# Key and value caches of a decode kernel: one queue with 64 KB rows, or two queues with 32 KB rows

## The chip, the cores and the metric

The kernel runs on one core of a Trainium2 chip. The metric is the device time of one execution in microseconds (us); lower is better.

## What is computed

One decoding step for a batch of 2: attention of 16 heads over a cache of 4096 positions with heads of 256, mixed by a gate with a small dense block. All is float32.

```
q = (x @ wq)                               # x: 2 x 448, wq: 448 x 4096
scores = q . k_cache * 256**-0.5           # per batch and head: 4096 scores
p = softmax(scores)
o = p . v_cache                            # per batch and head: 256 numbers
a = o @ wo                                 # wo: 4096 x 448
b = relu(x @ w1) @ w2                      # w1: 448 x 1792, w2: 1792 x 448
g = sigmoid((x * gate_w).sum())
out = g * a + (1 - g) * b
```

Each cache is 2 x 16 x 4096 x 256 float32, 134 MB. The two caches are nearly all of the 290 MB that the core reads.

## The kernel before

**Units.** The work is cut into U = 32 units, one for each pair of batch and head. Keys and values of a unit stand together in one input, `kv`: for each unit 128 rows (one for each partition of the on-chip memory) of SW = 16384 float32, which is 64 KB. The first half of a row is keys, the second half values. One DMA brings one unit, 8.39 MB.

**The ring.** On chip there are SLOTS = 3 buffers of 64 KB a partition (`ring`, `slot[0]` to `slot[2]`). Unit u goes to slot (u+1) % 3. Slot 0 first holds `wq` and the small inputs, then unit 2. At the end slot 0 takes `wm` (w1 and w2) after unit 29, and slot 1 takes `wo` after unit 30.

**The queue.** All DMAs are issued by SyncE (SP in the profile), in one queue: `wq`, unit 0, unit 1 at the start; unit 2 once the projections have read `wq` (semaphore `q_mm`); then unit u+3 each time unit u has been used up (semaphore `freed`, counted by VectorE), in a loop (L157 to L163) and written out at the end (L164 to L176). The last unit, 31, comes in two DMAs, keys first (L167, semaphore `slot_in[2]`) and values (L168, `last_v`). Then `wm` in two DMAs and `wo` in six.

**A unit's chain.** TensorE waits for the unit's slot (`slot_in`) and for its query (`queried`), and makes the scores with 32 matmuls of 128x512 (L131, `unit_pe`). VectorE takes the maximum (L351). ScalarE makes the exponentials and their sum (L318) and copies the next unit's query (L320, which releases `queried`). VectorE multiplies the eight blocks of values by the exponentials and adds up (L356), in place in the ring; the last of the eight adds 1 to `freed`. ScalarE copies the eight results (L323, `ov`). ScalarE's loop over units is L316 to L323.

**Start and end.** At the start ScalarE waits for `wq` on `slot_in[0]` (L296), spreads x, and TensorE makes the gate and the queries in two halves (L196 to L211). At the end TensorE has the hidden layer of the dense block (L111), the merge over units, w2 (L258), and `wo` in six blocks (L270, L283), each as it lands.

Each engine's instructions run in the order in which the code below issues them; the engines are held together by semaphores alone.

Of the kernel before, what the change touches and what calls it, by code (L numbers as in the profile page):

```python
# [7 lines left out]
ET = mybir.EngineType  # L8
# [4 lines left out]
SLOTS = 3  # L13
# [4 lines left out]

def gated_mix_decode(nc, wq, kv, wm, wo, out):
    U, _, SW = kv.shape  # L20
    D = 448
    B = 2
    RB = R // B
    T, DH = 2, 256
# [13 lines left out]
    pe, dve, act, pool, sp = nc.tensor, nc.vector, nc.scalar, nc.gpsimd, nc.sync  # L38
# [4 lines left out]
    def ev():  # L43
        sems.append(nc.alloc_semaphore(f"e{len(sems)}"))
        return sems[-1]
# [5 lines left out]
    slot = [ring[:, i * SW:(i + 1) * SW] for i in range(SLOTS)]  # L51

    def sb(name, *shape):
        t = nc.alloc_sbuf_tensor(name, list(shape), F32)
        assert nc.sbuf_base <= first
        return t.ap()
# [3 lines left out]

    out_sem = nc.alloc_semaphore("out_sem")
    slot_in = [ev() for _ in range(SLOTS)]
    last_v, w1_in, w2_in = ev(), ev(), ev()
    wo_in = [ev() for _ in ACC + DIRECT]
    scored, maxed, raised, queried, freed, kept = (ev() for _ in range(6))

    sp.dma_start(slot[0][:, :wq.shape[1]], wq).then_inc(slot_in[0], 16)
    sp.dma_start(slot[1], kv[0]).then_inc(slot_in[1], 16)
    sp.dma_start(slot[2], kv[1]).then_inc(slot_in[2], 16)

    ident = sb("ident", P, P)
    sel = sb("sel", P, R)
# [15 lines left out]
    p = sb("p", P, SG)  # L88
# [16 lines left out]
    def x_of(c, n=R):  # L105
        return xr[:, c].rearrange("p r b -> p (r b)")[:, :n]
# [17 lines left out]
    def unit_pe(k, u_wait, slot_wait, s):  # L124
        pe.wait_ge(slot_in[s], slot_wait)
        pe.wait_ge(queried, u_wait)
        for c in range(SG // CW):
            for t in range(T):
                for g in range(G):
                    lo = t * S + g * SG + c * CW  # L130
                    m = pe.matmul(sc[g * R:(g + 1) * R, c * CW:(c + 1) * CW],  # L131
                                  qc[:, s, t:t + 1].to_broadcast([P, R]), slot[s][:, lo:lo + CW],
                                  start=(t == 0), stop=(t == T - 1))
        m.then_inc(scored, 1)
# [5 lines left out]
    LOOP = -(-U // SLOTS)  # L140
# [10 lines left out]
    with nc.Block(no_gpsimd_drain=True) as block:  # L151

        @block.sync
        def _(_e):
            sp.wait_ge(q_mm, 2)
            sp.dma_start(slot[0], kv[2]).then_inc(slot_in[0], 16)
            with nc.Fori(0, LOOP - 2, engines=(ET.SP,)) as r:  # L157
                u0 = sp.snap(r * SLOTS)
                for k in range(SLOTS):
                    s = (k + 1) % SLOTS  # L160
                    sp.wait_ge(freed, u0 + k + 1)
                    sp.dma_start(slot[s], kv[bass.ds(u0 + k + SLOTS, 1)].rearrange("o p n -> (o p) n")  # L162
                                 ).then_inc(slot_in[s], 16)  # L163
            sp.wait_ge(freed, U - 4)  # L164
            sp.dma_start(slot[1], kv[U - 2]).then_inc(slot_in[1], 16)
            sp.wait_ge(freed, U - 3)
            sp.dma_start(slot[2][:, :SW // 2], kv[U - 1][:, :SW // 2]).then_inc(slot_in[2], 16)  # L167
            sp.dma_start(slot[2][:, SW // 2:], kv[U - 1][:, SW // 2:]).then_inc(last_v, 16)  # L168
            sp.wait_ge(freed, U - 2)
            sp.dma_start(w1, wm[:, :W1]).then_inc(w1_in, 16)  # L170
            sp.dma_start(w2, wm[:, W1:]).then_inc(w2_in, 16)
            sp.wait_ge(freed, U - 1)
            k = 0
            for n, s in zip(ACC + DIRECT, wo_in):
                sp.dma_start(w_o[:, k * D:(k + n) * D], wo[:, k * D:(k + n) * D]).then_inc(s, 16)  # L175
                k += n  # L176
            sp.wait_ge(res_ok, 1)
            sp.dma_start(out, res[0:7 * 15 + 1:7, :]).then_inc(out_sem, 16)
# [13 lines left out]
        def pe_main():  # L192
            pe.wait_ge(x_ok, 1)
            for c in range(KC):
                r = slice(0, P if c < KF else HP)
                m = pe.matmul(pa[:, :1], x_of(c, P) if c < KF else xn[r].rearrange("p r b -> p (r b)"), xg[r, c, B:],  # L196
                              start=(c == 0), stop=(c == KC - 1))
            m.then_inc(gate_mm, 1)
            W = 2 * KF * DH
            for i in range(2):  # L200
                if i:
                    pe.wait_ge(q_ok, i)
                project(pb, slot[0][:, i * NW // 2:(i + 1) * NW // 2], lambda c, g: g * W + c * CW,
                        lambda i: G * W + i * CW, CW, 0, KC).then_inc(q_mm, 1)
                pe.wait_ge(q_ok, i + 1)
                if i:
                    pe.wait_ge(qt_ok, i)
                else:
                    pe.wait_ge(ident_ok, 1)
                for k in range(2 * T):  # L210
                    m = pe.transpose(pc[:, k * P:(k + 1) * P], q[:, k * P:(k + 1) * P], ident)  # L211
                m.then_inc(q_tr, 1)
            with nc.Fori(0, LOOP, engines=(ET.PE,)) as r:
                u0 = pe.snap(r * SLOTS)

                def units(lo, hi):
                    for k in range(lo, hi):
                        unit_pe(k, u0 + (k + 1), r * 16 + (32 if k == SLOTS - 1 else 16), (k + 1) % SLOTS)

                units(0, FULL)  # L220
                with pe.If_lt(pe.to_reg(r), LOOP - 1):
                    units(FULL, SLOTS)
                pe.end_ifs()
# [69 lines left out]

        @block.scalar
        def _(_e):
            act.wait_ge(slot_in[0], 16)  # L296
            act.activation(xr, xg[:, :KF, None, :B].to_broadcast([P, KF, P // B, B]), AF.Copy)  # L297
            act.activation(xn, xg[:, KF:, :B].to_broadcast([P, P // B, B]), AF.Copy)
            act.wait_ge(xl_0, 1)
            for j in range(2):  # L300
                a = act.activation(xl[j * HP:(j + 1) * HP, j], xg[j * HP:(j + 1) * HP, KF:, :B]  # L301
                                   .to_broadcast([HP, RB, B]), AF.Copy)
            a.then_inc(x_ok, 1)
            act.wait_ge(gate_mm, 1)
            act.activation(ge, pa[:, :1], AF.Exp, scale=-1.0).then_inc(gate_ok, 1)  # L305
            for i in range(2):
                act.wait_ge(q_mm, i + 1)
                act.activation(q, pb, AF.Copy, scale=SCALE).then_inc(q_ok, 1)  # L308
                act.wait_ge(q_tr, i + 1)
                a = act.activation(qt[:, i * U // 2:(i + 1) * U // 2, :].rearrange("p (s n) t -> p s t n", s=2),  # L310
                                   pc.rearrange("p (s t x) -> p s t x", s=2, t=T)[:, :, :, ::17], AF.Copy)
                a.then_inc(qt_ok, 1)
            act.wait_ge(qt_ok, 2)
            act.activation(qc[:, 1, :], qt[:, 0, :], AF.Copy).then_inc(queried, 1)
            qf = qc.rearrange("p s t -> p (s t)")
            with nc.Fori(0, U, engines=(ET.Activation,)) as u:  # L316
                act.wait_ge(maxed, u + 1)
                act.activation(p, sc, AF.Exp, bias=nm[:, bass.ds(u, 1)], accum_out=ls[:, bass.ds(u, 1)]  # L318
                               ).then_inc(raised, 1)
                act.activation(qf[:, bass.ds((u + 2) % SLOTS * T, T)],  # L320
                               qt[:, bass.ds(u + 1, 1), :].rearrange("p o t -> p (o t)"), AF.Copy).then_inc(queried, 1)
                act.wait_ge(freed, u + 1)
                act.activation(ov[:, bass.ds(u, 1), :].rearrange("p o j -> p (o j)"), on, AF.Copy).then_inc(kept, 1)  # L323
            act.wait_ge(nb_ok, 1)
            act.activation(e, pc[:U, 0:P:R], AF.Exp, bias=nb, scale=-1.0).then_inc(e_ok, 1)
            act.wait_ge(hid_mm, 1)
            act.activation(hs, pa[:, :FG], AF.Relu, scale=omg).then_inc(hid_ok, 1)
            act.wait_ge(hid_tr, 1)
            act.activation(hr[:, :KF * G, :], pb[:, :KF * P].rearrange("p (k r) -> p k r", r=R), AF.Copy)
            for j in range(2):  # L330
                r = slice(j * HP, (j + 1) * HP)
                a = act.activation(hr[r, KF * G:, :],  # L332
                                   pb[r, KF * P + j * HP:KF * P + (j + 1) * HP].rearrange("p (k r) -> p k r", r=R),
                                   AF.Copy)
            a.then_inc(hr_ok, 1)
# [102 lines left out]
```

## Time and profile before

| | |
|---|---|
| median of 3 runs | 677.36 us (676.78 to 677.59) |
| the profiled execution's own time | 676.38 us |
| its span, first to last instruction | 674.8 us |
| bytes read | 289.54 MB, mean 429 GB/s over the span |
| DMA packets in SyncE's queue | 6080 |
| busy: TensorE, VectorE, ScalarE | 213.0, 339.8, 54.2 us |

The profile is one execution. Its page has the busy time of each engine, the span in 40 slices with the share of time that the 16 DMA engines were busy and the bytes that they moved, the chain of waits that ended last, groups of instructions by line, and the DMA issues. In the rows of an engine's instructions, the times are start and duration in us; in brackets is the idle time ahead and what ended it. A packet is one row of a DMA, or one write of 4 bytes that tells a semaphore that one DMA engine has done its share.

### The profile page before, as it was taken

The page shows a single profiled execution, that of the slowest core. Times are in us where ns is not written, and L with a number is a line of the kernel's source. Part 1 is how long each engine was busy: PE and PEld are TensorE (multiplying, and loading weights), DVE is VectorE, ACT ScalarE, POOL GpSimd, SP SyncE. Part 2 cuts the span into 40 slices and gives each one's busy share as a digit, 9 for nine tenths or more (in the row PEclk, how much of TensorE's full clock was granted, in tenths as well). Part 3 has the DMA queues.
Part 4 walks back from the last instruction along what each step waited for, and adds up shares of the span by engine and source line. Part 5 has one row for each costly group of instructions (what it writes and reads, how often), then busy time and mean ns, then how long its engine had stood idle before and what let it go on. Part 6 is the DMA issues. An engine that isn't in the chain of part 4 may idle for free.

```text
span 674.8 us, 4173 instructions
## 1 busy us (share of the span) xinstructions
PE 213.0 (32%) x1279; PEld 52.0 (8%) x1279; DVE 339.8 (50%) x561; ACT 54.2 (8%) x144; POOL 1.1 (0%) x9
## 2 busy tenths in 40 slices
PE   0633221333332123333321233333222333332455
PEld 0210000000000000000000000000000000000011
DVE  0024566545455665544656654455566445456670
ACT  0110000000000000000000000000000000000110
POOL 0000000000000000000000000000000000000000
PEclk9976567767655676776656677665667767655879
DMA  9999999999999999999999999999999999999997
GB/s 381 427 435 436 435 435 435 435 435 435 435 435 435 435 435 435 435 435 435 431 435 435 435 435 435 435 435 435 435 435 435 435 435 435 435 435 406 420 437 304
DMA packets 6082, 289.59 MB, mean 429 GB/s; under 512 B 704, under 2 KB 832, under 8 KB 1216
## 3 DMA queue, kind: packets, MB, share of 16 engines
q1 hardware_dynamic: 6080, 289.55, 99.3%
q8 instruction: 2, 0.03, 0.0%
HBM read 289.54 MB, written 0.01 MB: 429 GB/s over the span
## 4 chain that ended last, share of the span: by engine, by line
DMA 70%; DVE 12%; PE 9%; issue 6%; DVEq 1%; ACT 1%; SPq 0%; ACTq 0%
DMA ring<-in_kv 65%; DVE ring L356 10%; PE sc L131 9%; DMA ring<-in_wo 4%; DVE nm L351 2%; DVEq L356 1%; ACT p L318 1%; PE z L283 0%; DVEq L348 0%; DVEq L353 0%; PE acc L270 0%; SPq L175 0%; SPq L162 0%; DVEq L351 0%; DVE a_sb L375 0%
## 5 line engine op out<-in xcount | busy, mean ns | idle before, releaser
L356 DVE SCALAR_TENSOR_TENSOR ring<-ring,p 128x1024 f32 x256 | 295.9, 1222 | 54.8 <-ACT p L318 54.8
L131 PE MATMUL sc<-ring,qc 128*32 128x512 f32 x1024 | 182.6, 878 | 417.8 <-DMA ring<-in_kv 417.8
L351 DVE TENSOR_REDUCE nm<-sc 128x1024 f32 x32 | 39.2, 1225 | 236.1 <-PE sc L131 236.1
L131 PEld LDWEIGHTS sc<-ring,qc 128*32 128x32 f32 x1024 | 41.2, 154 | 558.6 <-issue 558.6
L318 ACT ACTIVATE p<-sc,nm 128x1024 f32<-128x1024 f32 x32 | 35.7, 1114 | 257.8 <-DVE nm L351 257.8
L323 ACT ACTIVATE ov<-on 128x8 f32 x32 | 6.7, 208 | 309.0 <-DVE ring L356 309.0
L356 DVE DVE_READ_ACCUMULATOR ring<-ring,p 128x1 f32 x256 | 21.4, 83 | 0.0
L343 DVE TENSOR_SCALAR ge<-ge 128x1 f32<-128x1 f32 x1 | 0.2, 155 | 21.5 <-ACT ge L305 21.5
L196 PE MATMUL pa<-ring,xr 128*128 128x1 f32 x6 | 1.4, 356 | 21.4 <-ACT xl L301 21.4
L375 DVE COPY a_sb<-acc 128x448 f32<-128x448 f32 x1 | 0.6, 625 | 14.7 <-PE acc L270 14.7
L111 PE MATMUL pa<-ring,xr 128*32 128x448 f32 x24 | 4.2, 830 | 11.7 <-DMA ring<-in_wm 11.7
L270 PE MATMUL acc<-ring,oc 128*32 128x448 f32 x52 | 5.9, 544 | 4.7 <-DMA ring<-in_wo 4.7
L111 PE MATMUL pb<-ring,xr 128*32 128x512 f32 x48 | 7.1, 737 | 0.0
L318 ACT ACTIVATION_READ_ACCUMULATOR p<-sc,nm x32 | 6.2, 193 | 0.0
L320 ACT ACTIVATE qc<-qt x32 | 6.1, 192 | 0.0
L258 PE MATMUL acc<-ring,hr 128*32 128x448 f32 x28 | 3.2, 541 | 1.0 <-ACT hr L332 1.0
L196 PEld LDWEIGHTS pa<-ring,xr 128*128 128x128 f32 x6 | 1.4, 326 | 21.4 <-ACT xl L301 21.4
L270 PEld LDWEIGHTS acc<-ring,oc 128*32 128x32 f32 x52 | 1.7, 109 | 8.9 <-issue 5.9
L114 PE MATMUL pb<-ring,xl 128*64 128x512 f32 x8 | 2.2, 618 | 0.0
L297 ACT ACTIVATE xr<-ring 128x384 f32<-128x384 f32 x1 | 0.5, 522 | 18.3 <-DMA ring<-in_wq 18.3
L111 PEld LDWEIGHTS pb<-ring,xr 128*32 128x32 f32 x48 | 1.6, 132 | 3.9 <-issue 3.9
L308 ACT ACTIVATE q<-pb 128x512 f32<-128x512 f32 x2 | 1.2, 598 | 8.6 <-PE pb L114 8.6
(56 smaller groups left out, 23.7 us busy)
## 6 DMA issues: line engine op xcount, KB each, us to landing
ring<-in_kv SPq DMA_DIRECT2D x2, 4096.0 KB, 34.7
ring<-in_wq SPq DMA_DIRECT2D x1, 7174.0 KB, 19.5
ring<-in_wm SPq DMA_DIRECT2D x2, 3136.0 KB, 30.7
ring<-in_wo SPq DMA_DIRECT2D x1, 3136.0 KB, 24.4
ring<-in_wo SPq DMA_DIRECT2D x1, 1792.0 KB, 28.3
ring<-in_wo SPq DMA_DIRECT2D x1, 896.0 KB, 30.0
ring<-in_wo SPq DMA_DIRECT2D x1, 672.0 KB, 31.1
ring<-in_kv SPq DMA_DIRECT2D x31, 39.6
```

Source lines behind the costliest of these rows:

```text
L111: m = pe.matmul(dst[g * R:(g + 1) * R, :n], x_of(c), w[:, at(c, g):at(c, g) + n], start=(c == 0), stop=False)
L114: m = pe.matmul(dst[i * HP:(i + 1) * HP, :n], xl.rearrange("p j r b -> p (j r b)"), w[:, at_last(i):at_last(i) + n], start=False, stop=True)
L131: m = pe.matmul(sc[g * R:(g + 1) * R, c * CW:(c + 1) * CW], qc[:, s, t:t + 1].to_broadcast([P, R]), slot[s][:, lo:lo + CW], start=(t == 0) ...
L196: m = pe.matmul(pa[:, :1], x_of(c, P) if c < KF else xn[r].rearrange("p r b -> p (r b)"), xg[r, c, B:], start=(c == 0), stop=(c == KC - 1))
L258: pe.matmul(acc[g * R:(g + 1) * R, :D], hr[:, k, :], w2[:, k * D:(k + 1) * D], start=(k < G), stop=False)
L270: m = pe.matmul(acc[g * R:(g + 1) * R, :D], o_of(k), w_o[:, k * D:(k + 1) * D], start=False, stop=(k >= n - G))
L308: act.activation(q, pb, AF.Copy, scale=SCALE).then_inc(q_ok, 1)
L318: act.activation(p, sc, AF.Exp, bias=nm[:, bass.ds(u, 1)], accum_out=ls[:, bass.ds(u, 1)]).then_inc(raised, 1)
L320: act.activation(qf[:, bass.ds((u + 2) % SLOTS * T, T)], qt[:, bass.ds(u + 1, 1), :].rearrange("p o t -> p (o t)"), AF.Copy).then_inc(quer ...
L323: act.activation(ov[:, bass.ds(u, 1), :].rearrange("p o j -> p (o j)"), on, AF.Copy).then_inc(kept, 1)
L351: dve.tensor_reduce(nm[:, bass.ds(u, 1)], sc, axis=AX.X, op=ALU.max, negate=True).then_inc(maxed, 1)
L356: m = dve.scalar_tensor_tensor(v, v, 1.0, p, op0=ALU.mult, op1=ALU.mult, accum_out=on[:, j:j + 1])
```

## The change

Keys and values of a unit become two DMAs. Keys of every unit stay in SyncE's queue; values of units 0 to 30 are issued by ScalarE, in ScalarE's own queue. Each DMA then has rows of 32 KB. Both count on the slot's semaphore, so that TensorE waits for 32 per unit and not 16. `wq` has a semaphore of its own (`wq_in`). ScalarE issues the values of units 0 and 1 when `wq` has landed, those of unit 2 behind the copy of the first query, and those of unit u+3 behind its copy of unit u's results (which waits for `freed`). Its loop is unrolled by three units. Of unit 31, the keys come in two DMAs with rows of 16 KB, and the values stay in SyncE's queue.

```diff
-    sp.dma_start(slot[0][:, :wq.shape[1]], wq).then_inc(slot_in[0], 16)
-    sp.dma_start(slot[1], kv[0]).then_inc(slot_in[1], 16)
-    sp.dma_start(slot[2], kv[1]).then_inc(slot_in[2], 16)
+    HW = SW // 2
+
+    def load(eng, u, s, at, n=HW):
+        rows = kv[u] if isinstance(u, int) else kv[bass.ds(u, 1)].rearrange("o p n -> (o p) n")
+        return eng.dma_start(slot[s][:, at:at + n], rows[:, at:at + n])
+
+    sp.dma_start(slot[0][:, :wq.shape[1]], wq).then_inc(wq_in, 16)
+    for u in range(SLOTS - 1):
+        load(sp, u, u + 1, 0).then_inc(slot_in[u + 1], 16)
...
                     sp.wait_ge(freed, u0 + k + 1)
-                    sp.dma_start(slot[s], kv[bass.ds(u0 + k + SLOTS, 1)].rearrange("o p n -> (o p) n")
-                                 ).then_inc(slot_in[s], 16)
+                    load(sp, u0 + k + SLOTS, s, 0).then_inc(slot_in[s], 16)
...
             sp.wait_ge(freed, U - 3)
-            sp.dma_start(slot[2][:, :SW // 2], kv[U - 1][:, :SW // 2]).then_inc(slot_in[2], 16)
-            sp.dma_start(slot[2][:, SW // 2:], kv[U - 1][:, SW // 2:]).then_inc(last_v, 16)
+            for i in range(2):
+                load(sp, U - 1, 2, i * HW // 2, HW // 2).then_inc(slot_in[2], 16)
+            load(sp, U - 1, 2, HW).then_inc(last_v, 16)
...
-            act.wait_ge(slot_in[0], 16)
+            act.wait_ge(wq_in, 16)
+            for u in range(SLOTS - 1):
+                load(act, u, u + 1, HW).then_inc(slot_in[u + 1], 16)
...
+            load(act, 2, 0, HW).then_inc(slot_in[0], 16)
+
+            def unit_act(u, at):
                 act.wait_ge(maxed, u + 1)
...
                 act.wait_ge(freed, u + 1)
                 act.activation(ov[:, bass.ds(u, 1), :].rearrange("p o j -> p (o j)"), on, AF.Copy).then_inc(kept, 1)
+
+            with nc.Fori(0, LOOP - 2, engines=(ET.Activation,)) as r:
+                u0 = act.snap(r * SLOTS)
+                for k in range(SLOTS):
+                    u, s = act.snap(u0 + k), (k + 1) % SLOTS
+                    unit_act(u, (k + 2) % SLOTS * T)
+                    load(act, u + SLOTS, s, HW).then_inc(slot_in[s], 16)
+            unit_act(U - 5, (U - 3) % SLOTS * T)
+            load(act, U - 2, 1, HW).then_inc(slot_in[1], 16)
+            with nc.Fori(U - 4, U, engines=(ET.Activation,)) as u:
+                unit_act(u, (u + 2) % SLOTS * T)
```

How the instructions stand on the two issuing engines follows. A row has the line, the operation, what it writes and reads, and the semaphores that it waits for, by number. Line numbers of the changed kernel are its own: L71 is the DMA in `load`. `ring_49` is the ring.

ScalarE, the start of its program, before. Semaphore e0 is `slot_in[0]`, on which `wq` lands, and e22 is POOL's clearing of `xl`:

```order
L297 ACT_TABLE_LOAD
L297 ACTIVATE xr<-ring 128x384 [waits e0]
L298 ACTIVATE xn<-ring 128x128
L301 ACTIVATE xl<-ring 64x32 [waits e22]
L301 ACTIVATE xl<-ring 64x32
```

The same place after. Semaphore e3 is `wq_in`, and e23 the former e22:

```order
L71 DMA ring_49<-in_kv 128x8192 [waits e3]
L71 DMA ring_49<-in_kv 128x8192
L305 ACT_TABLE_LOAD
L305 ACTIVATE xr<-ring_49 128x384
L306 ACTIVATE xn<-ring_49 128x128
L309 ACTIVATE xl<-ring_49 64x32 [waits e23]
```

Two DMAs now stand first and carry the wait for `wq`, and the load of the activation table, which stood ahead of that wait, is behind it.

ScalarE, one unit in its loop, before. Semaphore e13 is `maxed`, and e16 `freed`; ISA rows compute addresses:

```order
L318 ISA [waits e13]
L318 ACTIVATE p,ls<-sc,nm 128x1024
L320 ISA x2
L320 ACTIVATE qc<-qt 128x2
L323 ISA [waits e16]
L323 ACTIVATE ov<-on 128x8
```

The same unit after, the first of the three in the loop. Semaphore e14 is `maxed`, and e17 `freed`:

```order
L328 ISA [waits e14]
L328 ACTIVATE p,ls<-sc,nm 128x1024
L330 ISA
L330 ACTIVATE qc<-qt 128x2
L333 ISA [waits e17]
L333 ACTIVATE ov<-on 128x8
L71 ISA
L71 DMA ring_49<-in_kv 128x8192
```

The DMA of values stands behind the copy of the results and ahead of the next unit's wait for `maxed`.

SyncE, the end of the stream, before (e16 is `freed`):

```order
L165 DMA ring<-in_kv 128x16384 [waits e16]
L167 DMA ring<-in_kv 128x8192 [waits e16]
L168 DMA ring<-in_kv 128x8192
L170 DMA ring<-in_wm 128x6272 [waits e16]
L171 DMA ring<-in_wm 128x6272
```

And after (e17 is `freed`):

```order
L71 DMA ring<-in_kv 128x8192 [waits e17]
L71 DMA ring<-in_kv 128x4096 [waits e17]
L71 DMA ring<-in_kv 128x4096
L71 DMA ring<-in_kv 128x8192
L176 DMA ring<-in_wm 128x6272 [waits e17]
```

SyncE's order is as it was, with half of unit 30 gone to ScalarE and the keys of unit 31 in two pieces.

More of the change, by code (lines that the diff above doesn't have):

```diff
@@ L62, in gated_mix_decode @@
     slot_in = [ev() for _ in range(SLOTS)]
-    last_v, w1_in, w2_in = ev(), ev(), ev()
+    wq_in, last_v, w1_in, w2_in = (ev() for _ in range(4))
     wo_in = [ev() for _ in ACC + DIRECT]
     scored, maxed, raised, queried, freed, kept = (ev() for _ in range(6))
-    sp.dma_start(slot[0][:, :wq.shape[1]], wq).then_inc(slot_in[0], 16)
-    sp.dma_start(slot[1], kv[0]).then_inc(slot_in[1], 16)
-    sp.dma_start(slot[2], kv[1]).then_inc(slot_in[2], 16)
+    HW = SW // 2
[5 more added lines that the diff above has]
+        load(sp, u, u + 1, 0).then_inc(slot_in[u + 1], 16)
     ident = sb("ident", P, P)
@@ L155, in _ @@
             sp.wait_ge(q_mm, 2)
-            sp.dma_start(slot[0], kv[2]).then_inc(slot_in[0], 16)
+            load(sp, 2, 0, 0).then_inc(slot_in[0], 16)
             with nc.Fori(0, LOOP - 2, engines=(ET.SP,)) as r:
@@ L161, in _ @@
                     sp.wait_ge(freed, u0 + k + 1)
-                    sp.dma_start(slot[s], kv[bass.ds(u0 + k + SLOTS, 1)].rearrange("o p n -> (o p) n")
-                                 ).then_inc(slot_in[s], 16)
+                    load(sp, u0 + k + SLOTS, s, 0).then_inc(slot_in[s], 16)
             sp.wait_ge(freed, U - 4)
-            sp.dma_start(slot[1], kv[U - 2]).then_inc(slot_in[1], 16)
+            load(sp, U - 2, 1, 0).then_inc(slot_in[1], 16)
             sp.wait_ge(freed, U - 3)
-            sp.dma_start(slot[2][:, :SW // 2], kv[U - 1][:, :SW // 2]).then_inc(slot_in[2], 16)
-            sp.dma_start(slot[2][:, SW // 2:], kv[U - 1][:, SW // 2:]).then_inc(last_v, 16)
+            for i in range(2):
+                load(sp, U - 1, 2, i * HW // 2, HW // 2).then_inc(slot_in[2], 16)
+            load(sp, U - 1, 2, HW).then_inc(last_v, 16)
             sp.wait_ge(freed, U - 2)
@@ L217, in units @@
                     for k in range(lo, hi):
-                        unit_pe(k, u0 + (k + 1), r * 16 + (32 if k == SLOTS - 1 else 16), (k + 1) % SLOTS)
+                        unit_pe(k, u0 + (k + 1), r * 32 + 32, (k + 1) % SLOTS)
                 units(0, FULL)
@@ L315, in _ @@
             qf = qc.rearrange("p s t -> p (s t)")
-            with nc.Fori(0, U, engines=(ET.Activation,)) as u:
+            load(act, 2, 0, HW).then_inc(slot_in[0], 16)
+            def unit_act(u, at):
                 act.wait_ge(maxed, u + 1)
@@ L319, in _ @@
                                ).then_inc(raised, 1)
-                act.activation(qf[:, bass.ds((u + 2) % SLOTS * T, T)],
+                act.activation(qf[:, bass.ds(at, T)],
                                qt[:, bass.ds(u + 1, 1), :].rearrange("p o t -> p (o t)"), AF.Copy).then_inc(queried, 1)
```

## The prediction

> **What bounds the kernel now.** I read the page's slices and DMA part first, then its chain of waits.
>
> ```profile
> span 674.8 us, 4173 instructions
> ...
> GB/s 381 427 435 436 435 435 435 435 435 435 435 435 435 435 435 435 435 435 435 431 435 435 435 435 435 435 435 435 435 435 435 435 435 435 435 435 406 420 437 304
> ...
> q1 hardware_dynamic: 6080, 289.55, 99.3%
> q8 instruction: 2, 0.03, 0.0%
> ...
> DMA 70%; DVE 12%; PE 9%; issue 6%; DVEq 1%; ACT 1%; SPq 0%; ACTq 0%
> ```
>
> The packets of one queue fill 99.3% of 16 DMA engines' span, at 435 GB/s in nearly every slice: 289.55 MB at that rate are 665.6 us of a span of 674.8. The chain's VectorE and TensorE shares are a unit's use between two landings; whether the stream ever waits for it shows in one unit's rows, in order of time.
>
> ```profile
> 543.27 6.32 PE L131 MATMUL sc<-ring,qc 128*32 128x512 f32 x32 [13.57 <-DMA ring<-in_kv]
> ...
> 551.13 1.11 ACT L318 ACTIVATE p<-sc,nm 128x1024 f32<-128x1024 f32 x1 [8.72 <-DVE nm L351]
> ...
> 562.09 0.21 ACT L323 ACTIVATE ov<-on 128x8 f32 x1 [9.66 <-DVE ring L356]
> 562.13 0.33 SPq L162 DMA_DIRECT2D ring<-in_kv  x1
> ```
>
> A unit lands, TensorE starts at 543.27, and the slot is given back and refilled at 562.13, 18.9 us later. Another line's group of DMAs gives what is queued then.
>
> ```profile
> DMA to landing us min/median/max: 39.0/39.6/40.8
> ```
>
> The 27 loads of L162 land 39.6 us after issue, two units' worth: at each issue a whole unit is still queued, so issue times have some 19 us to spare and the stream never runs dry. The kernel is bound by its DMA engines, which are at their rate; a change can only alter time per byte or packet, the start, or the end.
>
> **Part 1: more packets.** Each load of 64 KB rows gives each DMA engine 8 rows and 1 completion, 9 packets (6080 packets hold 128 + 16 for each such load). Halving adds 9 per engine for each of units 0 to 30, and splitting the keys of unit 31 adds 9 more: 32 x 9 = 288 on top of 6080/16 = 380, in all 10688 packets. What does a packet cost beside its bytes? Unit 31 already comes in 32 KB rows, so the starts of TensorE near the end compare both sizes.
>
> ```profile
> 601.23 6.35 PE L131 MATMUL sc<-ring,qc 128*32 128x512 f32 x32 [13.57 <-DMA ring<-in_kv]
> 620.53 5.24 PE L131 MATMUL sc<-ring,qc 128*32 128x512 f32 x32 [12.95 <-DMA ring<-in_kv]
> 630.19 5.34 PE L131 MATMUL sc<-ring,qc 128*32 128x512 f32 x32 [4.42 <-DMA ring<-in_kv]
> ```
>
> All three wait for the DMA. A unit in 64 KB rows took 620.53 - 601.23 = 19.30, the keys of unit 31, half the bytes in as many rows, 630.19 - 620.53 = 9.66. Twice that is 19.32, so nine more packets cost 0.02 us, with 0.02 of rounding on either side: 0 to 0.04. From the other side, the packets' own time is 99.3% of 674.8 = 670.1 us, 4.4 more than the bytes at 435 GB/s. Put wholly on the 380 packets that is 11.6 ns each, 0.10 for nine; but slow first rows (381 GB/s in the first slice) are in it, so it is an upper end. I take 0.04, the end of the nearer row that leans towards the other bound: 32 x 0.04 = +1.3 us, ends 0 and 32 x 0.10 = +3.3. All of it is on the path, since the DMA engines have no idle time to hide it in.
>
> The Trainium skill, "DMA: Bandwidth & Descriptors", section "Why small descriptors are slow (HBM only)", gives a fixed overhead of about 3 cycles for each packet inside a DMA engine, whatever queue it came from. An estimate from that page, at its 850 MHz: 288 x 3.5 ns = 1.0 us. By it the sum would be 0.3 us lower; the trace's 0 to 0.04 per nine packets agrees.
>
> **Part 2: ScalarE issues values.** SyncE's issue takes 0.33 us (562.13 above), and ScalarE's 31 issues should be alike. In the loop it comes behind the 0.21 us copy, and ScalarE is then idle 8.72 us till the next maximum, so it is off ScalarE's path; values are queued about 0.5 us after keys, against 19 us to spare. Cost 0. If that cover went, it would be 0.33 per unit. SyncE's issues stay as many, each with fewer bytes; 0.
>
> **Part 3: the start.** The rows:
>
> ```profile
> 0.72 1.28 ACT L297 ACT_TABLE_LOAD   x1 [0.72 <-PEq L427]
> ...
> 20.28 0.52 ACT L297 ACTIVATE xr<-ring 128x384 f32<-128x384 f32 x1 [18.28 <-DMA ring<-in_wq]
> ...
> 33.76 0.33 SPq L156 DMA_DIRECT2D ring<-in_kv  x1
> ...
> 35.34 0.20 ACT L314 ACTIVATE qc<-qt 128x2 f32<-128x2 f32 x1
> ...
> 39.72 5.51 PE L131 MATMUL sc<-ring,qc 128*32 128x512 f32 x32 [4.65 <-DMA ring<-in_kv]
> ```
>
> Behind the wait for `wq` at 20.28 now come two issues (some 0.7 us) and the table load (1.28): 2.0 us later for x, the projections, unit 2's issue (33.76, to 35.8, with units 0 and 1 still queued till 59) and the first query (35.54, to 37.5, needed at 39.72). All hidden; without the 4.18 us of cover it would be 2.0. Meanwhile SyncE's queue holds keys 0 and 1, so the engines don't idle till ScalarE's first issue takes hold. But keys get a lead: one or two rows of 1.2 us (9.66 / 8) pass before values join, and the lead stays, since both queues then always hold work. Every unit's last values land 1.2 to 2.4 us later than now, and TensorE, which waits for both halves, starts that much later.
>
> **Part 4: the end.** That lag moves unit 30's release, and with it the issue of `wo`, and the merge:
>
> ```profile
> 638.18 2.70 SPq L175 DMA_DIRECT2D ring<-in_wo  x6
> ...
> 647.26 3.21 PE L111 MATMUL pa<-ring,xr 128*32 128x448 f32 x16 [11.73 <-DMA ring<-in_wm]
> ...
> 656.25 3.20 PE L258 MATMUL acc<-ring,hr 128*32 128x448 f32 x28 [1.01 <-ACT hr L332]
> 662.72 3.20 PE L270 MATMUL acc<-ring,oc 128*32 128x448 f32 x28 [3.27 <-DMA ring<-in_wo]
> ...
> 669.02 0.96 PE L270 MATMUL acc<-ring,oc 128*32 128x448 f32 x8 [0.43 <-DMA ring<-in_wo]
> ```
>
> `wo` issued at 640.6 still finds w1 (landed at 647) and w2 queued. TensorE waits 3.27 us for the first block of `wo`, so a merge up to 2.4 us late still ends first. Cost 0, with 0.9 us left.
>
> **Sum.** 676.38 (profiled) + 1.3 = 677.7. The median stands 0.98 above the profiled execution, so I forecast 678.6; with the packets' ends, 677.4 to 680.7.
>
> **Rivals.**
>
> *Changing queues costs a DMA engine time (slower).* Before, one queue's rows follow each other; now an engine goes back and forth, 16 changes per unit, 496 in all. The trace has one place like it, one of the two q8 packets of 16 KB, which falls in the stretch from 58.9 to 79.3:
>
> ```profile
> 39.60:58.90 19.30, 5.51 (x32) 1.27 (x32) 10.48 (x17) 1.50 (x4) 0.00 (x0) 0.68 1.00 435
> 58.90:79.30 20.40, 6.09 (x32) 1.32 (x32) 10.48 (x17) 1.50 (x4) 0.00 (x0) 0.58 0.95 412
> ```
>
> The last two columns are the DMA share and GB/s. That unit took 20.40 and not 19.30: 1.1 us for 16 KB, whose bytes are 0.6 at one engine's 435/16 GB/s. The 0.5 left over are two changes, 0.25 each. At that price 496 changes are +124 us, 801; but that packet came singly, while the two streams here queue far ahead. A third such packet, for ScalarE's longer program (63 rows, before 27), would cost up to 1.1; I take none. Priced like a row's start (0.04/9 us), the 496 changes are +2.2: 680.8. Beside the 1.3 of part 1, any price above 0.1 ns a change, (1.35 - 1.3)/496, makes it slower. Against: 8 rows a unit at 435 GB/s leave no sign of a gap between rows.
>
> *Two queues overlap the starts of rows (faster).* While one row ends, the other queue's is ready. It would take away what 380 packets now pay, 380 x 0.04/9 = 1.7 us, and the 1.3 isn't spent: 675.7; at the 11.6 ns end, 673.0. Against: the rate stands at 435 in slice after slice, like a ceiling.
>
> *Rows cost nothing and the queue doesn't matter.* The lower end of part 1: 677.4. The Trainium skill, "DMA: Bandwidth & Descriptors", section "Issuing engines are not separate DMA queues", speaks for this and against the change: queues of several engines end on the same 16 DMA engines, so a second one saves only issue time. Every issue of this trace is hidden, which agrees; two loading queues at once are in no run yet.
>
> *Unequal shares (slower).* If SyncE's queue went first, values 30 would land behind w2, at about 647.1 (w1's landing, by L111) + 7.4 (448 x 1792 float32 at 435 GB/s) = 654.5; the slot would be free 17.7 later (620.53 to 638.18), at 672.2, and `wo` (4096 x 448 float32, 16.9 us) would land near 689 where its last blocks now land at 669: +20, 697. It decides once values lag more than the 3.27 us above.
>
> **How the numbers follow.** Clean sharing with paid rows 0.53 (678.6; its own range 677.4 to 680.7), free rows 0.15, queue changes 0.17, overlap 0.11, unequal shares 0.04. About 0.2%, 1.35 us, is what a measurement of this kernel tells from no change: faster is below 676.0, slower above 678.7. Faster: nearly all of overlap, 0.10. Free rows, and a good half of the likeliest case, are same: 0.44. The rest, 0.46, is slower. The range leaves out most of overlap, unequal shares and the upper part of queue changes: 675.9 to 683.5.
>
> **What would show it.** The page: two queues of near-equal bytes, 10688 packets in all, 434 to 435 GB/s in the middle slices; TensorE starts 0.02 to 0.10 us further apart per unit; table load and first query 2 us later; TensorE still waiting for `wo` at L270's counterpart. It is wrong if the unit interval grows by over 0.1 us (queue changes) or falls below 19.30 (overlap), or if unit 30 lands over 3 us later than now.

## The result, and the profile after

The changed kernel is slower by a quarter of a per cent: 678.32 us (677.14 to 679.5, 19 runs) against 676.69 (675.83 to 677.59, 19 runs) of the kernel before, a ratio of 1.0026 with a 95% interval of 1.0019 to 1.0032, which is +1.3 to +2.2 us. The forecast was 678.6. One of ten executions in the changed kernel's later set took 723.53 us, in a slower state, and is left out of that set's numbers.

The page of the changed kernel (677.92 us by itself, span 676.6), the parts that answer to those shown of before; q10 is ScalarE's queue:

```profile
span 676.6 us, 4173 instructions
...
GB/s 380 426 434 434 433 434 434 434 434 434 434 434 434 434 434 434 434 434 434 434 434 434 434 434 434 434 434 434 432 434 434 432 432 434 430 431 420 432 442 281
...
q1 hardware_dynamic: 6224, 159.53, 54.8%
q10 hardware_dynamic: 4464, 130.03, 44.5%
q8 instruction: 3, 0.05, 0.0%
...
DMA 69%; DVE 12%; PE 10%; issue 7%; DVEq 1%; ACT 1%; ACTq 0%; SPq 0%
```

Two queues together hold 6224 + 4464 = 10688 packets, and the plateau stands at 434 GB/s where it stood at 435. The DMA engines are as full as before, at a rate that is lower by a fraction of a per cent.

TensorE's starts of a unit's scores in the changed kernel, in order of time (unit 0, unit 3 and unit 29):

```profile
43.30 4.95 PE L137 MATMUL sc<-ring,qc 128*32 128x512 f32 x32 [5.94 <-DMA ring<-in_kv]
...
102.44 6.10 PE L137 MATMUL sc<-ring,qc 128*32 128x512 f32 x32 [13.79 <-DMA ring<-in_kv]
...
605.84 5.29 PE L137 MATMUL sc<-ring,qc 128*32 128x512 f32 x32 [12.96 <-DMA ring<-in_kv]
```

and unit 3 of the kernel before, whose unit 29 started at 601.23:

```profile
98.70 5.04 PE L131 MATMUL sc<-ring,qc 128*32 128x512 f32 x32 [13.15 <-DMA ring<-in_kv]
```

All wait for the DMA. From unit 3 to unit 29 are 26 intervals: (601.23 - 98.70) / 26 = 19.328 us before, (605.84 - 102.44) / 26 = 19.362 after, 0.034 more per unit. The first unit starts 3.58 us later (before: 39.72), and that lag stays through the stream: with the packets' share on top, unit 29 starts 4.61 us later.

The start in ScalarE's rows, which has the two issues and then the table load behind the wait for `wq`:

```profile
20.21 0.88 ACTq L71 DMA_DIRECT2D ring<-in_kv  x2
21.12 1.28 ACT L305 ACT_TABLE_LOAD   x1 [21.12 <-DMA ring<-in_wq]
22.42 0.52 ACT L305 ACTIVATE xr<-ring 128x384 f32<-128x384 f32 x1
...
37.64 0.20 ACT L322 ACTIVATE qc<-qt 128x2 f32<-128x2 f32 x1
```

The first query is ready 2.3 us later than before, and no one waits for it, since the first unit now lands at 43.2.

The DMA queues in two stretches of the changed kernel, from 19.2 to 24.1 us, and from 24.1 to 29:

```profile
q1 hardware_dynamic: 80, 2.10, 99.4%
...
q1 hardware_dynamic: 32, 1.05, 49.5%
q10 hardware_dynamic: 32, 1.05, 49.5%
```

In the first, SyncE's queue alone starts 80 packets: 16 tell that `wq` has landed, 64 are key rows, four for each engine. Only then do values begin, some four us after ScalarE's first issue, and from there on the two queues share row by row. So keys lead by four rows. Why ScalarE's first row comes that late is not shown.

The end in TensorE's rows:

```profile
623.35 5.06 PE L137 MATMUL sc<-ring,qc 128*32 128x512 f32 x32 [12.23 <-DMA ring<-in_kv]
...
648.33 3.22 PE L117 MATMUL pa<-ring,xr 128*32 128x448 f32 x16 [13.38 <-DMA ring<-in_wm]
652.95 0.39 PE L240 MATMUL pc<-ident,nm 128*32 128x128 f32 x1 [1.41 <-DVE ring L377]
...
659.96 4.52 PE L264 MATMUL acc<-ring,hr 128*32 128x448 f32 x26 [1.02 <-ACT hr L353]
...
664.35 5.15 PE L276 MATMUL acc<-ring,oc 128*32 128x448 f32 x42
669.92 0.96 PE L276 MATMUL acc<-ring,oc 128*32 128x448 f32 x8 [0.42 <-DMA ring<-in_wo]
```

Unit 30 lands 2.8 us later than before, though unit 29 landed 4.6 later. The queues' packets next to each other show why, from 617.0 to 620.4 us, when the keys of unit 31 come in rows of 16 KB beside the values of unit 30 in rows of 32 KB:

```profile
q10 hardware_dynamic: 32, 1.05, 71.4%
q1 hardware_dynamic: 32, 0.51, 34.8%
```

The two queues take turns by the row and not by the byte, so the queue with the longer rows gets twice the bytes, and the last values of unit 30 catch up by 1.8 us. Unit 30 starts 17.51 us after unit 29 here; it is 19.39 in the kernel without the lead below, where hardly any such rows meet, and 15.69 with twice the lead, where more of them do.

TensorE no longer waits for the first blocks of `wo`. Its w2 matmuls (L264, L258 before) start 3.7 us later (659.96 against 656.25), and 26 of them take 4.52 us where 28 took 3.20. Only the last block of the first three is still waited for, 0.42 us, as before, and it comes 0.90 later (669.02 before). So in this execution TensorE is not later at the end than `wo` makes it. The rest of the 1.8 us by which this execution's span is longer lies behind the last matmul, and differs from run to run: SyncE's wait for the output's DMA was 1.5 us here and 0.5 in the profile before.

### The profile page after: what moved, and what is told of

Read it like the earlier page. It is cut to its first block, busy times and chain, and to the rows that moved or that the text cites. A ratio compares the mean times of both kernels' runs of the same rounds, so it can differ in the third digit from the quotient of the medians.

```text
span 676.6 us, 4173 instructions
## 1 busy us (share of the span) xinstructions
PE 214.9 (32%) x1279; PEld 52.8 (8%) x1279; DVE 339.8 (50%) x561; ACT 54.2 (8%) x144; POOL 1.1 (0%) x9
## 3 DMA queue, kind: packets, MB, share of 16 engines
q1 hardware_dynamic: 6224, 159.53, 54.8%
q10 hardware_dynamic: 4464, 130.03, 44.5%
## 4 chain that ended last, share of the span: by engine, by line
DMA 69%; DVE 12%; PE 10%; issue 7%; DVEq 1%; ACT 1%; ACTq 0%; SPq 0%
DMA ring<-in_kv 62%; DVE ring L377 10%; PE sc L137 10%; DMA ring<-in_wo 4%; DMA ring<-in_wq 3%; DVE nm L372 2%; DVEq L377 1%; ACT p L328 1%; PE z L289 0%; DVEq L369 0%; DVEq L374 0%; PE acc L276 0%; SPq L181 0%; ACT ov L333 0%; DVEq L372 0%
## 5 line engine op out<-in xcount | busy, mean ns | idle before, releaser
L333 ACT ACTIVATE ov<-on 128x8 f32 (+1 forms) x32 | 6.7, 208 | 308.9 <-DVE ring L377 308.9
L328 ACT ACTIVATION_READ_ACCUMULATOR p<-sc,nm (+1 forms) x32 | 6.2, 193 | 0.0
L330 ACT ACTIVATE qc<-qt 128x2 f32 (+2 forms) x32 | 6.2, 192 | 0.0
L264 PE MATMUL acc<-ring,hr 128*32 128x448 f32 x28 | 4.9, 808 | 1.0 <-ACT hr L353 1.0
L393 DVE COPY oc<-pc 128x256 f32<-128x256 f32 x4 | 1.4, 417 | 1.4 <-PE pc L251 1.4
```

The source lines that it names most:

```text
L264: pe.matmul(acc[g * R:(g + 1) * R, :D], hr[:, k, :], w2[:, k * D:(k + 1) * D], start=(k < G), stop=False)
L330: act.activation(qf[:, bass.ds(at, T)], qt[:, bass.ds(u + 1, 1), :].rearrange("p o t -> p (o t)"), AF.Copy).then_inc(queried, 1)
L393: m = dve.tensor_copy(oc[:, h], oc_of(h))
```

## The experiments

Theories: *packets*, that a packet costs 4 to 5 ns beside its bytes, in any queue; *queues*, that going back and forth costs time, or saves it; *lead*, that the keys' lead uses up the cover at the end; *program*, that ScalarE's longer program costs, through one more instruction packet.

### 32 KB rows in one queue

Based on the changed kernel; ScalarE issues nothing and has its old loop.

```diff
                     load(sp, u0 + k + SLOTS, s, 0, slot_in[s])
+                    load(sp, u0 + k + SLOTS, s, HW, slot_in[s])
...
-                    load(act, u + SLOTS, s, HW, slot_in[s])
```

> All rows of 32 KB as in the changed kernel, 10688 packets, but in SyncE's queue alone (keys, then values, of each unit). Packet theory (a packet costs 4 to 5 ns beside its bytes, whatever its queue): 1.2 to 1.4 us slower than before, and within 0.5 us of the changed kernel; a third instruction packet of 16 KB only if TensorE's program brings it. Queue theory (going back and forth between two queues is what costs): as fast as before, 676.7, and 1.6 us faster than the changed kernel. Units land one after the other, so the first scores start at 39.7 and not at 43.3.

677.39 us (677.06 to 678.34) beside 676.13 of the kernel before: ratio 1.0019 (1.0010 to 1.0028), +1.3 us. Its packets, in one queue, and its units 3 and 29:

```profile
q1 hardware_dynamic: 10688, 289.56, 99.3%
```

```profile
98.68 5.12 PE L143 MATMUL sc<-ring,qc 128*32 128x512 f32 x32 [13.07 <-DMA ring<-in_kv]
...
602.07 6.01 PE L143 MATMUL sc<-ring,qc 128*32 128x512 f32 x32 [13.88 <-DMA ring<-in_kv]
```

(602.07 - 98.68) / 26 = 19.361 us per unit, with two queues 19.362. The rows alone give the interval; the second queue adds nothing to it. Queues, as a cost in the stream, falls.

### Rows of 8 KB, in one queue and in two

`load` in four pieces for each half unit, TensorE's wait four times as high. The two kernels differ in who issues the values.

```diff
+        w = n // pieces
+        for i in range(pieces):
+            lo = at + i * w
+            eng.dma_start(slot[s][:, lo:lo + w], rows[:, lo:lo + w]).then_inc(sem, 16)
```

> SyncE's queue alone, every half unit in four DMAs with rows of 8 KB: 2016 packets more for each DMA engine than before. Packet theory at 4.4 ns: 9.0 us slower than before, 685.7 (4 to 5 ns: 684.8 to 686.8). If a row's start cost nothing and the loss came from elsewhere: 676.7.

> As one_queue_8k, but values through ScalarE's queue: some 64 changes of queue per unit and DMA engine, 1984 in all. Packet theory: within 0.5 us of one_queue_8k, plus what the keys' lead costs at the end (0 to 1). Queue theory, a price for each change: 5 ns would make it 10 us slower than one_queue_8k, 1 ns 2 us. If two queues hide row starts: up to 9 us faster than one_queue_8k.

One queue: 685.75 us, +9.6 on 676.13, ratio 1.0138 (1.0123 to 1.0154). Two queues: 687.40 (685.59 to 687.89), +11.3, ratio 1.0157 (1.0141 to 1.0172). Units 3 and 29 of the first, then of the second:

```profile
99.71 6.46 PE L143 MATMUL sc<-ring,qc 128*32 128x512 f32 x32 [13.57 <-DMA ring<-in_kv]
...
609.93 5.65 PE L143 MATMUL sc<-ring,qc 128*32 128x512 f32 x32 [14.40 <-DMA ring<-in_kv]
```

```profile
104.17 5.78 PE L142 MATMUL sc<-ring,qc 128*32 128x512 f32 x32 [14.27 <-DMA ring<-in_kv]
...
614.39 4.96 PE L142 MATMUL sc<-ring,qc 128*32 128x512 f32 x32 [13.39 <-DMA ring<-in_kv]
```

510.22 us for 26 units in both, 19.624 each, to the hundredth of a microsecond, though the second goes from queue to queue some 64 times per unit. Against 19.328 that is 0.296 for 63 packets, 4.7 ns each; by the time, 9.6 / 2016 = 4.8 ns. Packets holds at seven times the change's size, and going back and forth costs nothing that these intervals show, nor does it hide a row's start. The 63 packets are 56 rows and 7 completions; what each kind costs by itself is not shown. The Trainium skill's rule that queues of several engines end on the same 16 DMA engines, and that a second one saves only the time of issuing ("DMA: Bandwidth & Descriptors", section "Issuing engines are not separate DMA queues"), agrees with this.

The 1.7 us between the two kernels are a little more than the packets theory allowed (0.5, and up to 1 for the lead). They are not in the stream, but behind it, in TensorE's rows at the end, one queue first:

```profile
671.49 6.40 PE L285 MATMUL acc<-ring,oc 128*32 128x448 f32 x44 [2.20 <-DMA ring<-in_wo]
678.31 0.96 PE L285 MATMUL acc<-ring,oc 128*32 128x448 f32 x8 [0.42 <-DMA ring<-in_wo]
```

```profile
675.56 5.77 PE L281 MATMUL acc<-ring,oc 128*32 128x448 f32 x50
```

With two queues TensorE comes to `wo` when all of its first three blocks are there, and is the last to finish. That is what lead says, but not lead alone: the w2 matmuls ahead of it took 5.02 us for 26 in this execution, and 3.20 for 28 in the one with one queue. How much of the 1.7 us each has is not shown; the times with two queues reach from 685.59, as fast as with one, to 687.89.

### No lead

`wq` in two halves, one through each queue, with values 0 and 1 behind it in ScalarE's.

```diff
+    sp.dma_start(slot[0][:, :WH], wq[:, :WH]).then_inc(wq_in, 16)
+    act.dma_start(slot[0][:, WH:2 * WH], wq[:, WH:]).then_inc(wq_in, 16)
+    for u in range(SLOTS - 1):
+        load(sp, u, u + 1, 0, slot_in[u + 1])
+        load(act, u, u + 1, HW, slot_in[u + 1])
```

> Two queues as in the changed kernel, but wq comes half through each, with values 0 and 1 behind it in ScalarE's queue from the start: keys get no lead, and the table load is early again. Theory that the lead costs at the end (values 3.6 us late use up the 3.3 us that TensorE waited for wo): 0.3 to 1.0 us faster than the changed kernel. Packet theory alone: within 0.3 us of the changed kernel. In both the first scores start near 39.8, keys and values of a unit land within a row (1.2 us) of each other, and TensorE waits for wo again.

677.45 us (677.15 to 679.0), ratio 1.0019 (1.0010 to 1.0028). Unit 0 and the end of its profile:

```profile
40.06 5.77 PE L145 MATMUL sc<-ring,qc 128*32 128x512 f32 x32 [4.39 <-DMA ring<-in_kv]
...
657.41 3.20 PE L272 MATMUL acc<-ring,hr 128*32 128x448 f32 x28 [1.01 <-ACT hr L359]
663.49 3.20 PE L284 MATMUL acc<-ring,oc 128*32 128x448 f32 x28 [2.88 <-DMA ring<-in_wo]
```

The lag is gone (40.06), and TensorE waits for `wo` again in this execution. It costs what 32 KB rows cost in one queue. To set it beside the changed kernel on one chip, both ran again:

> The changed kernel once more, beside the next three on the same chip. Packet theory: 1.2 to 1.4 us slower than before. Theory that the keys' lead costs at the end as well: 1.6 to 2.0 us slower, its times spread over more than 2 us, since TensorE then sets the end with a clock that differs from run to run.

> The kernel without the keys' lead once more, beside the changed one. Packet theory alone: as fast as the changed kernel, within 0.2 us. Lead theory: 0.3 to 0.7 us faster than it.

The changed kernel took 677.94 us (677.34 to 678.90), ratio 1.0022 (1.0012 to 1.0031), the one without the lead 677.53, ratio 1.0020 (1.0012 to 1.0029). The changed kernel is 1.5 us slower than before, between what the two theories said (1.2 to 1.4, and 1.6 to 2.0). Without the lead it is 0.4 us faster by the medians, with intervals that overlap: a gain of the expected sign that these times don't make certain. The spread of the changed kernel was 1.6 us, less than expected.

The spans, first to last instruction, which are on record for every execution, tell more. On this chip their medians are 676.4 us with the lead and 675.7 without. Of the changed kernel's 28 executions in both sets 15 have a span above 676.2 us, up to 678.2; of the 33 without a lead (twice this kernel, once 32 KB rows in one queue) one has, at 677.1. On the chip where both ran again it is five of nine against one of eleven. So the lead costs something in about half of the executions, and little in the others. The line at 676.2 was drawn after seeing the spans.

A missing wait for `wo` is no sign of the lead by itself. In the second profile of the kernel without the lead the matmuls of `wo`'s first three blocks have none either, nor in a profile with the loads of before, that of "The longer program" below:

```profile
659.88 5.44 PE L272 MATMUL acc<-ring,hr 128*32 128x448 f32 x26 [1.01 <-ACT hr L359]
...
665.12 6.07 PE L284 MATMUL acc<-ring,oc 128*32 128x448 f32 x50
```

```profile
658.26 5.44 PE L258 MATMUL acc<-ring,hr 128*32 128x448 f32 x26 [1.01 <-ACT hr L334]
...
663.50 6.13 PE L270 MATMUL acc<-ring,oc 128*32 128x448 f32 x50
```

From 658 to 664 us TensorE's granted clock was 0.50 and 0.52 in these two, and 1.00 in the profile before. So the 3.27 us of cover in the profile before are those of an execution with the full clock; at a clock near 0.5 they were gone without any lead.

### Twice the lead

ScalarE issues values 0 and 1 behind the gate's exponential.

```diff
             act.activation(ge, pa[:, :1], AF.Exp, scale=-1.0).then_inc(gate_ok, 1)
+            for u in range(SLOTS - 1):
+                load(act, u, u + 1, HW).then_inc(slot_in[u + 1], 16)
```

> As the changed kernel, but ScalarE issues the values of units 0 and 1 some 3.3 us later, behind the gate's exponential, so that keys lead by about 7 rows and not 4 and each unit lands some 3.3 us later still. Packet theory alone: as fast as the changed kernel, within 0.3 us. Lead theory: with the cover at the end used up, 2.5 to 3.3 us slower than the changed kernel, and the blocks of wo are all there when TensorE comes to them. In both the unit interval stays 19.36.

678.37 us, ratio 1.0038 (1.0025 to 1.0051), but in two groups: five runs from 677.19 to 678.37, four from 679.92 to 680.53. Neither theory had that. In its profile, of the first group (677.41), unit 0 starts at

```profile
47.93 5.78 PE L137 MATMUL sc<-ring,qc 128*32 128x512 f32 x32 [11.80 <-DMA ring<-in_kv]
```

4.63 us later than in the changed kernel. From unit 2 on it is 3.60 (86.73 against 83.13), near the 3.3 expected; what held unit 0 up by another microsecond is not shown. The end:

```profile
655.28 0.40 PE L240 MATMUL pc<-ident,nm 128*32 128x128 f32 x1 [3.76 <-DVE ring L377]
...
662.46 2.83 PE L264 MATMUL acc<-ring,hr 128*32 128x448 f32 x26 [1.01 <-ACT hr L353]
...
665.15 5.77 PE L276 MATMUL acc<-ring,oc 128*32 128x448 f32 x50
```

The merge starts 2.3 us later than in the changed kernel (652.95), yet the w2 matmuls of L264 take 2.83 us for 26, where the changed kernel took 4.52, and time is made up. Busy time of each engine in the stretch from 658 to 664 us, of this kernel, of the changed one, and of the changed one when it ran again, with the granted TensorE clock as the third number from the right:

```profile
658.00:664.00 6.00, 4.54 (x39) 1.69 (x41) 1.84 (x5) 1.44 (x4) 0.00 (x0) 0.84 0.93 399
```

```profile
658.00:664.00 6.00, 4.95 (x35) 2.01 (x39) 1.03 (x4) 0.81 (x3) 0.00 (x0) 0.72 0.94 402
```

```profile
658.00:664.00 6.00, 4.62 (x31) 1.67 (x31) 1.42 (x4) 1.45 (x4) 0.00 (x0) 0.50 0.94 404
```

At a clock of 0.50 the w2 matmuls of the changed kernel, run again, took 5.05 us, and its execution 678.90 us; VectorE began the copy of the result at 675.18, against 673.59 in the changed kernel's first profile. Without the lead, a clock of 0.50 and not 1.00 in that stretch moved the copy by less, from 673.46 to 673.92. So in these profiles the lead shows where TensorE's granted clock in the last 20 us is low. Two more executions were profiled for the slower group:

> The kernel with values 3.3 us later once more, for a profile: its times fell into two groups, 677.2 to 678.4 and 679.9 to 680.5 us, and the profile seen was of the first. Theory that TensorE's granted clock near the end decides: a profile of the second group shows a clock near 0.5 in the stretch from 658 to 670 us, where the first had 0.84 and then 1.00, with the w2 matmuls (L264) taking over 4.5 us for 26 where the first took 2.8, and no wait for wo. Theory that the DMA stream is what differs: the same clock as before, and the last blocks of wo landing 2 us later.

> The same once more, for a second chance of a profile of the slower group; expectations as for the look ahead of it.

They took 677.59 and 678.20 us, the first group again, so no profile of the slower group exists, and what sets the groups apart is not shown. Two things speak for the clock. Over the whole execution the four of the slower group had a mean granted clock of 0.650 to 0.658, and the five others 0.657 to 0.674; but in the first 19 executions of the changed kernel the mean clock doesn't go with the span (678.2 us at 0.668, 675.5 at 0.667). And an estimate from two profiles fits: the merge here starts at 655.28, 0.90 later than in the changed kernel run again (654.38, span 677.4), which makes 678.3, and the slower group's spans are 678.3 to 678.9. The second of the two executions had one thing more: at 1.8 us SyncE's wait for the output's DMA was 1.3 longer than in the profile of before, with a third q8 packet in the trace at the same time.

### The longer program

The kernel before, with ScalarE's loop unrolled by eight.

```diff
-            with nc.Fori(0, U, engines=(ET.Activation,)) as u:
+            with nc.Fori(0, U // 8, engines=(ET.Activation,)) as r:
+                for k in range(8):
+                    u = act.snap(r * 8 + k)
```

> The kernel before with ScalarE's loop unrolled by eight: a program of 68 rows (before 27, changed kernel 63), no DMA added or moved. Theory that the longer program costs: a third instruction packet of 16 KB near the end, and 0.3 to 1.0 us slower than before. Packet theory: as fast as before, within 0.2 us, with or without that packet.

676.69 us beside 676.40, ratio 1.0005 (0.9996 to 1.0014), with the packet:

```profile
q8 instruction: 3, 0.05, 0.0%
```

The third packet is there, and no cost that these runs make certain: +0.3 us by the medians is the low end of what the program theory said, and the interval, -0.3 to +0.9 us, holds both theories. The kernels with 32 KB rows speak against a cost: the one without the lead, with ScalarE's long program, took 677.45 us beside 677.39 with the short one in one queue. That a long program always brings the packet is not so: the profile of twice the lead, with a program as long as the changed kernel's, has two. In a single execution the packet can cost: where it falls beside the output's DMA, SyncE's wait for that DMA was 1.5 us (the changed kernel) and 1.8 (the second of the two executions above), and 0.6 where it had passed (the changed kernel run again).

## Why the prediction was right, point by point

- **More packets: right, in count and price.** 10688 packets came. The price was taken as 0.04 us for nine, 4.4 ns each; the intervals show 0.034 against the profile before, 0.044 against that of the longer program, whose loads are the same (from 98.67 to 600.92 us, 19.317 each), and rows of 8 KB, where it is large, give 4.7 to 4.8 ns. In one queue the rows alone cost 1.3 us, as forecast. The estimate of 3.5 ns from the Trainium skill ("DMA: Bandwidth & Descriptors", section "Why small descriptors are slow (HBM only)"), 1.0 us, was somewhat low. Of the two bounds, the comparison of 19.30 with 2 x 9.66 was the one to trust, but it gave 0 to 0.04 and no more: that its upper end was taken was a judgement that came out. The other, 11.6 ns, held more than packets: the first slice ran at 381 GB/s.
- **Issue by ScalarE: right.** Its 31 issues took 0.33 to 0.46 us each, and unit intervals are the same with and without them.
- **The start: right in what is hidden, wrong in one size.** The query came 2.3 us later (forecast 2.0), unseen. But keys lead by four rows and not by one or two: ScalarE's first row came some 4 us after its issue, where I had reckoned with 1.2 to 2.4. Each unit of the stream landed 3.6 us later for it, not 1.2 to 2.4.
- **The end: the step that failed, by a little.** "Cost 0, with 0.9 us left" took the cover of 3.27 us from one execution with the full clock. At a clock of 0.52 it was gone with the loads of before too, w2 taking 5.4 us and not 3.2; and unit 30 came 2.8 us later, not 2.4 at most. Cost: 0.4 us by the medians of the kernels with and without the lead, 0.7 by those of their spans; nothing in an execution like the first profile of the changed kernel. That the clock decides between these rests on a few profiles.
- **The rivals.** Queue changes have no price: 64 a unit leave the interval equal to 0.01 us in 510. The 0.25 us read from an instruction packet was not a price of changing queues, and the sum of 801 us left out the packets' 1.3. Overlap of row starts falls by the same number. Free rows falls, at 9.6 us for 8 KB rows. Unequal shares falls for rows of one size, which alternate one by one; where the sizes differ, at unit 31's keys, shares are unequal in bytes, and that helped.

So +1.76 by the ratio is 1.3 of packets and some 0.4 of lead, with a rest within the noise. That 678.6 lies so near 678.32 is in part luck: the median of three on which it stands, 677.36, was 0.67 above that of all 19, and the forecast of the change, 1.3, was some 0.4 short; the two misses have opposite signs. Of the signs of being wrong that the prediction named none came, but one nearly: unit 30 landed 2.8 us late, 623.35 against 620.53, and not over 3, only because of the 16 KB rows beside it; unit 29 was 4.6 late.

## What to carry to other kernels

A stream that already fills its DMA engines gains nothing from a second queue; what counts here is the number of packets, some 4 to 5 ns on each DMA engine for every row or completion (4.7 with rows of 8 KB), whichever queue it is in. So keep rows as long as the layout allows, and multiply the extra packets per engine before splitting a load. When two queues must join, give both the same amount of work ahead of the first joint load: the one that starts first kept its lead here as long as both had rows of the same size, and every wait for both halves ended that much later. Before trusting a cover at the end, see more than one execution: what TensorE has to spare depends on the clock that it is granted.

## What the runs showed of the hardware that I had not expected

- Two queues on the same DMA engines took turns row by row, at no price: from 24.1 to 29 us each started 32 rows, and over 26 units one and two queues took the same 510.22 us with 8 KB rows. The turns go by the row, not by the byte: with rows of 32 KB in one queue and 16 KB in the other, 32 rows each moved 1.05 and 0.51 MB.
- A DMA issued into a second queue while the first was busy started late: some 4 us from ScalarE's issue at 20.21 to its first row, by which time the other queue was four rows ahead.
- The clock that TensorE is granted from 658 to 664 us ranged from 0.50 to 1.00 between profiles, also between two of one kernel (without the lead: 1.00, then 0.50). The w2 matmuls took 3.20 us for 28 in the first, and 5.44 for 26 in the second. The end of the execution moved little there (0.5 us), and more where the lead came on top.
- An instruction packet of 16 KB in queue q8 near the end went with a wait for the 7 KB output that was 1.0 to 1.3 us longer in the two profiles where it fell beside that DMA.
